# One core, attention twice and an MLP: the hand-written order of steps replaced by another, and the output tiles in a pool of five buffers

## The chip, the cores and the metric

The kernel runs on one core of one Trainium2 chip. The metric is the device time of one execution in microseconds (us), median over runs. TensorE is called PE here, VectorE DVE, ScalarE ACT, GpSimd POOL and SyncE SP.

## What is computed

Eight batches with eight heads each, 576 rows per batch. A small set of 32 rows `p` per head first attends to the keys and values; its result then serves as keys and values for all 576 rows of `q`. The result, 4608 x 512, goes through an MLP with a hidden width of 2048.

```python
def sm_attn(qq, kk, vv):
    s = scale * np.matmul(qq, kk.transpose(0, 1, 3, 2))
    s = s - np.max(s, axis=-1, keepdims=True)
    a = np.exp(s)
    a = a / (np.sum(a, axis=-1, keepdims=True) + 1e-09)
    return np.matmul(a, vv)
p_packed = sm_attn(p, k, v)
out = sm_attn(q, p_packed, p_packed)
...
h = x @ w_in
r = np.maximum(h, 0.0)
g = s * (r * r) + b
return (g @ w_out).astype(np.float32)
```

## The kernel before

The work is cut into steps, each a small function, and a long string of words (lines 581 to 614) says in which order the steps are written into the program. A word is a letter, a batch and, where there are parts, a part. All instructions are pinned: each engine runs its own in the order of the words and waits, in order, for what an instruction needs. The words, with what PE does in each:

- `Lk`, `Lv`, `Lq`, `Lwi`, `Lwo`, `Lpall`, `Lsb` load from HBM through POOL's queue (lines 108 to 140). `kn`, `vn` and `qn` have one buffer each, so the load of a batch waits until the one before has been used up.
- `Tk`, `Tq` (batches 0 and 1) transpose k and q on PE, half a batch each, 12 matmuls, and DVE copies the result out. `Dk`, `Dq` (batches 2 to 7) do it by a DMA transpose in SP's queue instead (line 204), from `kn` and `qn` into `kT` and `qT`.
- `V` reorders `vn` into `vr` on DVE. `PP` and `PPA` bring `p` of batch 0 and of the others into `pbd`.
- `F` (a=0, 1) are the first scores, 12 matmuls out of `kT`, and an exp on ACT. `P` (two halves, 18 small matmuls each) multiplies by `vr`; after the second half DVE and ACT copy the result by turns into `ppd`. `S` are the second scores, 16 matmuls, with two exps on ACT.
- `A` (two) makes the softmax weights `aT`: 2 matmuls, `ld` and `rcd` on ACT, one product on DVE. `W` multiplies the small attention result by W_in (16 matmuls, 8 in batch 0); ACT and DVE each evacuate one half into `pw`.
- `M` (16 per batch, `h` are halves of one) is the MLP's first layer: 4 matmuls out of `pw` and `aT`, a relu on ACT (in batch 0, every fourth on DVE, line 399), the square into `gT` on DVE.
- `O b.t xn` does n of the 16 matmuls of output tile t of batch b; after the last one DVE writes `ysb` (line 451) and SP stores it with two DMAs. `B` are 16 matmuls of the bias. `Z` are matmuls on zeros that nobody reads.

Two places matter for the order. PSUM has two buffers `hps` (line 57) through which all of T, F, P, S, A, W and M go in turn: the next step but one waits until ACT or DVE have read the tile. `ysb` comes from a pool with three buffers (line 55): the fourth tile to be written waits until the store of the first has landed.

```python
ysp = ctx.enter_context(tc.tile_pool(name="ysp", bufs=3))
psh = ctx.enter_context(tc.tile_pool(name="psh", bufs=2, space=bass.MemoryType.PSUM))
...
self.ysb = ysp.tile([P, NB], F32, tag="ysb", name="ysb")
```

Of the kernel before, what the change touches and what calls it, by code (L numbers as in the profile page):

```python
# [14 lines left out]
def kernel(  # L15
# [565 lines left out]
    for word in """
        Lwi3 Lwi0 Lwi2 Lwi1 Lwo0 Lwo1 Lpall Tk0.0 Z3 Tk0.1 Lk1 Lwo2 Lsb PP0 V0.0 Z6 F0.0 V0.1 Z4 F0.1
        Tq0.0 P0.0 P0.1 Tq0.1 Lq1 Lv1 Lwo3 Z5 S0 Z7 A0.0 Z1 W0.0 Z6 A0.1 Z1 h0.0.0 h0.1.0 Z6 h0.0.1
        h0.1.1 Z1 W0.1 M0.2 W0.2 B0-3 M0.3 B3-4 W0.3 O0.0x3 M0.4 B4-8 PPA M0.5 O0.0x2 O0.1x5 O0.2x3
        Tk1.1 M0.6 B8-12 Tk1.0 Lk2 M0.7 O0.0x2 F1.0 Tq1.0 O0.0x1 O0.1x1 M0.8 O0.1x1 Tq1.1 V1 Lv2 Lq2
        O0.1x1 F1.1 O0.0x1 O0.1x1 M0.9 O0.2x2 P1.0 P1.1 B12-16 S1 O0.0x1 O0.1x1 O0.2x2 M0.10 A1.0 O0.2x3
        W1.0 O0.0x1 O0.1x1 O0.2x1 V2 O0.3x3 M0.11 O0.3x3 A1.1 W1.2 O0.0x1 Dq2 Dk2 Lk3 Lv3 Lq3 O0.1x1
        O0.2x1 O0.3x2 M0.12 O0.3x2 M1.0 O0.3x2 M0.13 O0.0x1 M1.1 O0.1x1 O0.2x1 M0.14 O0.0x1 O0.1x1 M1.2
        O0.2x1 O0.3x1 M0.15 F2.0 O0.0x1 O0.1x1 M1.3 F2.1 O0.0x1 O0.1x1 O0.2x2 M1.4 P2.0 O0.3x1 P2.1
        O0.3x2 O1.0x1 M1.5 O1.0x1 S2 O1.0x4 O1.1x1 V3 M1.6 O1.1x1 A2.0 O1.1x2 W2.0 O1.0x1 O1.1x3 O1.2x1  # L590
        M1.7 Dq3 Dk3 Lk4 Lv4 Lq4 O1.2x3 A2.1 W2.2 O1.0x1 O1.1x1 O1.2x4 M1.8 O1.3x3 M2.0 O1.3x1 M1.9
        O1.0x1 O1.1x1 M2.1 F3.0 O1.0x1 O1.1x1 M1.10 O1.2x1 M2.2 O1.2x1 F3.1 O1.0x1 M1.11 O1.1x1 O1.2x1
        M2.3 P3.0 P3.1 M1.12 O1.0x1 O1.1x1 O1.2x1 S3 O1.3x1 O1.0x1 O1.1x1 V4 O1.2x1 O1.3x1 M2.4 O1.3x1
        M1.13 O1.3x3 M1.14 M2.5 Dq4 Dk4 Lk5 Lv5 Lq5 O1.0x1 O1.1x1 O1.2x1 O1.3x1 M1.15 M2.6 O1.0x1 O1.1x1
        O1.2x1 O1.3x1 W3.0 O1.0x1 O1.1x1 O1.2x1 O1.3x3 M2.7 A3.0 O1.3x1 O1.4x2 W3.2 O1.4x6 M2.8 O1.4x5
        A3.1 F4.0 O1.4x2 M2.9 O1.4x1 O2.0x3 F4.1 O2.0x1 M3.0 O2.0x1 M2.10 O2.0x1 P4.0 O2.0x1 P4.1 M2.11
        O2.0x1 S4 V5 O2.0x4 M2.12 Dq5 Dk5 Lk6 Lv6 Lq6 M3.1 O2.1x3 M2.13 O2.0x1 M3.2 O2.1x3 M2.14 O2.0x1
        M3.3 O2.1x3 M2.15 O2.0x1 M3.4 O2.1x2 F5.0 A4.0 O2.0x1 O2.1x3 W4.0 O2.1x2 O2.2x4 A4.1 O2.2x7 W4.2
        O2.2x5 M4.0 F5.1 O2.3x2 M3.5 O2.3x1 P5.0 O2.3x1 M4.1 P5.1 O2.3x3 Dq6 Dk6 Lk7 O2.3x3 V6 Lv7 Lq7
        O2.3x1 M4.2 M3.6 O2.3x2 S5 O2.3x3 O3.0x1 M4.3 O3.0x1 M3.7 O3.0x3 M4.4 O3.0x1 M3.8 O3.0x1 F6.0  # L600
        O3.0x1 M4.5 O3.0x1 M3.9 F6.1 O3.1x2 M4.6 O3.0x1 M3.10 O3.1x1 P6.0 M4.7 P6.1 O3.0x1 O3.1x6 M3.11
        V7 O3.1x2 M4.8 O3.2x2 M3.12 O3.0x1 O3.1x1 M4.9 M3.13 Dq7 Dk7 O3.0x1 O3.1x1 O3.2x2 M4.10 M3.14
        O3.0x1 O3.1x1 O3.2x2 M4.11 O3.2x1 M3.15 O3.0x1 O3.1x1 O3.2x1 M4.12 O3.2x1 A5.0 O3.0x1 O3.1x1
        W5.0 O3.2x6 M4.13 O3.2x1 O3.3x8 W5.2 O3.3x6 A5.1 M4.14 O3.3x2 F7.0 O3.4x5 S6 O3.4x5 F7.1 O3.4x5
        P7.0 O3.4x1 P7.1 M5.0 O4.0x7 M5.1 O4.0x7 M5.2 O4.0x1 M4.15 O4.1x3 M5.3 O4.1x1 A6.0 O4.0x1 O4.1x1
        W6.0 O4.1x5 M5.4 O4.1x6 A6.1 M5.5 O4.2x7 S7 O4.2x4 M6.0 O4.2x2 M5.6 O4.2x2 M6.1 O4.2x1 O4.3x1
        M5.7 O4.3x2 M6.2 O4.3x3 M5.8 O4.3x1 M6.3 O4.3x3 M5.9 O4.3x1 M6.4 O4.3x3 M5.10 M6.5 O4.3x2 O5.0x1
        M5.11 M6.6 O5.0x3 M5.12 M6.7 O5.0x3 M5.13 O5.0x6 M5.14 O5.0x1 O5.1x5 M5.15 O5.0x1 O5.1x5 A7.0
        O5.0x1 O5.1x6 W7.0 O5.2x13 W7.2 O5.2x3 O5.3x16 W6.2 O5.4x7 M6.8 O5.4x7 M6.9 O5.4x2 A7.1 O6.0x3
        M6.10 O6.0x6 M7.0 M6.11 O6.0x2 O6.1x2 M7.1 O6.1x1 M6.12 O6.0x1 O6.1x1 M7.2 M6.13 O6.0x1 O6.1x2  # L610
        M7.3 M6.14 O6.0x1 O6.1x2 M7.4 O6.1x1 M6.15 O6.0x1 O6.1x2 M7.5 O6.1x1 O6.0x1 O6.1x4 O6.2x1 M7.6
        O6.2x7 M7.7 O6.2x5 M7.8 O6.2x3 O6.3x2 M7.9 M7.10 O6.3x3 M7.11 M7.12 O6.3x6 M7.13 O6.3x5 O7.0x2
        M7.14 O7.0x7 M7.15 O7.0x6 O7.1x1 O7.0x1 O7.1x15 O7.2x16 O7.3x16 O7.4x16
    """.split():
# [31 lines left out]
```

## Time and profile before

| | us |
|---|---|
| median of 3 runs (288.86 to 289.34) | 288.96 |
| the profiled execution | 288.51 |
| its span, from the first to the last instruction | 286.7 |
| PE busy in it | 252.0 (88%) |
| ACT busy | 148.5 (52%) |
| DVE busy | 143.4 (50%) |

PE is the engine to look at; the others are about half used. The mean busy share hides what happens in time: PE works without a gap from about 187 us to the end, and has gaps before. Its clock was granted in full except in two of the 40 slices of the page, at about 72 to 79 and 136 to 143 us, after the two longest gaps. What has to be read, then, is each place where a matmul waits, what ended that wait, and what PE does from the start of one step to the start of the next.

### The profile page before, as it was taken

Reading aid. Unit: us, or ns where it says so; the run is one execution under the profiler, and the core shown is the slowest. Engines: PE = TensorE matmul, PEld = TensorE weight load, DVE = VectorE, ACT = ScalarE, POOL = GpSimd, SP = SyncE. Lnnn points to the kernel's source line nnn. Section 1 sums busy time; section 2 is a strip of 40 time slices with the busy share of each in tenths; the row PEclk is TensorE's granted clock in tenths of the full one; section 3 lists DMA queues with packets and bytes.
Section 4 is the critical chain, followed back from the end, with each engine's and each line's share of the span. In section 5 each row is a group of like instructions: output and inputs, shape, how many; then the busy total and the mean of one; then the engine's idle time right before and its main releaser. Section 6 shows DMA issues by size and latency. Waiting matters only on the chain.

```text
span 286.7 us, 5273 instructions
## 1 busy us (share of the span) xinstructions
PE 252.0 (88%) x2143; PEld 140.3 (49%) x2182; DVE 143.4 (50%) x274; ACT 148.5 (52%) x229; POOL 29.7 (10%) x44
## 2 busy tenths in 40 slices
...
PEclk9999999999699999999699999999999999999999
...
GB/s 79 182 206 207 195 203 161 143 164 118 259 123 80 203 143 173 222 87 164 121 235 121 155 183 130 129 64 30 74 39 37 0 112 48 26 75 37 64 85 73
DMA packets 59209, 35.48 MB, mean 124 GB/s; under 512 B 31920, under 2 KB 54704, under 8 KB 59184
## 3 DMA queue, kind: packets, MB, share of 16 engines
...
## 4 chain that ended last, share of the span: by engine, by line
PE 62%; DMA 20%; ACT 7%; DVE 6%; issue 3%; POOL 1%; SPq 1%; POOLq 0%; ACTq 0%; DVEq 0%
PE yps L61 34%; PE hps L61 25%; DMA vn<-in_v_dram 8%; DMA kT<-kn 7%; ACT rlu L72 3%; DMA out_dram<-ysb 2%; DMA kn<-in_k_dram 2%; PE zps L61 2%; DVE gT L72 1%; PE hps L64 1%; ACT pw L72 1%; ACT ld L72 1%; DVE pw L72 1%; DVE pbd L72 1%; DVE ysb L72 1%
## 5 line engine op out<-in xcount | busy, mean ns | idle before, releaser
L61 PE MATMUL yps<-w_out_sb,gT 128*128 128x512 bf16 (+1 forms) x559 | 144.7, 379 | 8.5 <-DVE gT L72 6.7
L72 ACT ACTIVATE rlu<-hps 128x576 bf16<-128x576 f32 x122 | 78.1, 651 | 58.1 <-PE hps L61 50.2
L72 DVE TENSOR_TENSOR gT<-rlu 128x576 bf16<-128x576 bf16 x126 | 57.3, 457 | 67.9 <-ACT rlu L72 66.4
L61 PEld LDWEIGHTS <-gT 128*128 128x128 bf16 x592 | 55.4, 99 | 57.4 <-DVE gT L72 9.5
L61 PE MATMUL hps<-aT,pw 128*128 128x288 bf16 x512 | 82.1, 287 | 0.7 <-DVE pw L72 0.2
L61 PEld LDWEIGHTS <-pw 128*128 128x128 bf16 x512 | 49.7, 98 | 32.6 <-issue 4.2
L72 DVE SCALAR_TENSOR_TENSOR ysb<-yps,svec,biasrep 128x512 f32<-128x512 f32 (+1 forms) x37 | 26.5, 733 | 23.7 <-PE yps L61 16.8
L72 ACT ACTIVATE pw<-hps,rd 128x1024 bf16<-128x1024 f32 (+1 forms) x18 | 18.4, 1020 | 13.3 <-PE hps L61 13.1
...
L72 DVE TENSOR_TENSOR aT<-e,rcd 128x576 bf16<-128x576 bf16 x16 | 12.1, 758 | 23.5 <-ACT rcd L72 21.7
L72 DVE TENSOR_SCALAR pw<-hps,rd 128x1024 bf16<-128x1024 f32 (+1 forms) x18 | 20.9, 1161 | 2.3 <-PE hps L61 1.2
...
L61 PE MATMUL hps<-pbd,kT 128*128 128x64 bf16 x192 | 8.5, 196 | 9.0 <-DMA kT<-kn 7.1
L61 PE MATMUL zps<-zb 128*128 128x512 bf16 x49 | 14.3, 427 | 1.4 <-DVE zb L72 1.2
L61 PE MATMUL hps<-w_in_sb,ppd 64*32 64x512 bf16 x256 | 13.1, 405 | 2.5 <-DVE pw L72 1.0
...
L61 PEld LDWEIGHTS <-kT 128*128 128x128 bf16 x192 | 7.7, 100 | 12.7 <-DMA kT<-kn 8.2
L72 ACT ACTIVATE ld<-hps 128x576 f32<-128x576 f32 x16 | 10.4, 650 | 6.6 <-PE hps L61 6.6
L72 ACT ACTIVATE e<-hps,rs 128x576 bf16<-128x576 f32 (+1 forms) x18 | 11.3, 686 | 1.5 <-PE hps L61 1.5
...
L72 ACT ACTIVATE rcd<-ld 128x576 f32<-128x576 f32 x16 | 11.0, 685 | 0.5
L72 ACT CAST ppd<-hps 64x128 bf16<-64x128 f32 x16 | 4.2, 261 | 12.9 <-DVE ppd L72 12.1
...
## 6 DMA issues: line engine op xcount, KB each, us to landing
...
qn<-in_q_dram POOLq DMA_DIRECT2D x7, 576.0 KB, 13.2
...
```

The costliest lines, as they stand in the source:

```text
L61: return tc.keep_in_program_order(nc.tensor.matmul(*a, **kw))
L64: return tc.keep_in_program_order(nc.tensor.transpose(*a, **kw))
L72: return lambda *a, **kw: tc.keep_in_program_order(f(*a, **kw))
```

## The change

Three things. The string of words is another one, with the same steps in another order and other numbers of `Z` (59 matmuls on zeros in place of 52). `ysb` gets a pool of its own with five buffers. The order of the first loads differs. The steps themselves are unchanged.

```diff
     ysp = ctx.enter_context(tc.tile_pool(name="ysp", bufs=3))
+    outp = ctx.enter_context(tc.tile_pool(name="outp", bufs=5))
...
-                self.ysb = ysp.tile([P, NB], F32, tag="ysb", name="ysb")
+                self.ysb = outp.tile([P, NB], F32, tag="ysb", name="ysb")
...
-        Lwi3 Lwi0 Lwi2 Lwi1 Lwo0 Lwo1 Lpall Tk0.0 Z3 Tk0.1 Lk1 Lwo2 Lsb PP0 V0.0 Z6 F0.0 V0.1 Z4 F0.1
-        Tq0.0 P0.0 P0.1 Tq0.1 Lq1 Lv1 Lwo3 Z5 S0 Z7 A0.0 Z1 W0.0 Z6 A0.1 Z1 h0.0.0 h0.1.0 Z6 h0.0.1
...
+        Lwi1 Lwi0 Lwo0 Lwi2 Lwi3 Lwo2 Lwo1 Lpall Tk0.0 Z10 Tk0.1 PP0 Z6 F0.0 V0.0 F0.1 V0.1 Z5 P0.0
+        Tq0.0 P0.1 Z4 Tq0.1 Lq1 Lk1 Lwo3 Lv1 Lsb Z3 S0 Z7 A0.0 A0.1 Z2 W0.0 Z3 W0.1 B0-4 Z7 h0.0.0
...
-        O2.0x1 S4 V5 O2.0x4 M2.12 Dq5 Dk5 Lk6 Lv6 Lq6 M3.1 O2.1x3 M2.13 O2.0x1 M3.2 O2.1x3 M2.14 O2.0x1
-        M3.3 O2.1x3 M2.15 O2.0x1 M3.4 O2.1x2 F5.0 A4.0 O2.0x1 O2.1x3 W4.0 O2.1x2 O2.2x4 A4.1 O2.2x7 W4.2
...
+        O2.3x3 W4.0 O2.3x4 W4.2 V5 O2.3x6 S4 O2.3x3 O3.0x1 A4.0 O3.0x2 A4.1 O3.0x2 Dq5 Dk5 Lk6 Lv6 Lq6
+        M3.15 O3.0x10 M4.0 M4.1 O3.0x1 O3.1x1 M4.2 M4.3 O3.1x2 M4.4 M4.5 O3.1x2 M4.6 M4.7 O3.1x2 M4.8
+        F5.0 O3.1x2 F5.1 O3.1x1 M4.9 O3.1x2 P5.0 M4.10 P5.1 O3.1x4 O3.2x3 W5.0 O3.2x6 W5.2 O3.2x6 S5
```

For batches 2, 4 and 5 both `W` now stand ahead of `S`, with output steps between; `Dq` and `Dk` of the next batch come after `A`; then the `M` come two at a time with two output steps between pairs, and `F` of the next batch stands near the end of that row. For batches 0, 1, 3, 6 and 7 the steps are spread in other ways.

SP's queue from its start. Before, the first transposes (`qT`, `kT` of batch 2) stood ahead of all stores of output tiles (`out_dram<-ysb`):

```order
L72 DMA_TRANSPOSE qT_87<-qn 128x24x96
L72 DMA_TRANSPOSE kT_85<-kn 128x24x96
L72 DMA out_dram<-ysb 96x512
L72 DMA out_dram<-ysb 32x512
L72 DMA out_dram<-ysb 64x512 x2
```

Now the same queue from its start:

```order
L73 DMA out_dram<-ysb 96x512
L73 DMA out_dram<-ysb 32x512
L73 DMA out_dram<-ysb 64x512 x2
L73 DMA out_dram<-ysb 32x512
L73 DMA out_dram<-ysb 96x512
L73 DMA_TRANSPOSE qT_90<-qn 128x24x96
L73 DMA_TRANSPOSE kT_88<-kn 128x24x96
```

The transposes of batch 2 have moved behind the six stores of the first three output tiles.

DVE around `P2`, `S2` and `V3` (`rd`, `ppd`, `rs` are what follows `P2`; `vr` is `V3`). Before:

```order
L72 SCALAR_TENSOR_TENSOR ysb<-yps,svec,biasrep 128x512 x3
L72 TENSOR_TENSOR gT<-rlu 128x576
L72 RECIPROCAL rd<-hps 128x2
L72 CAST ppd_90<-hps 64x128 x2
L72 TENSOR_SCALAR rs<-rd 128x2
L72 SCALAR_TENSOR_TENSOR ysb<-yps,svec,biasrep 128x512
L72 TENSOR_TENSOR gT<-rlu 128x576
L72 COPY vr<-vn 96x8x6x64
```

Now the same place:

```order
L73 TENSOR_TENSOR gT<-rlu 128x576 x11
L73 RECIPROCAL rd<-hps 128x2
L73 CAST ppd_93<-hps 64x128 x2
L73 TENSOR_SCALAR rs<-rd 128x2
L73 TENSOR_SCALAR pw<-hps,rd 128x1024 x2
L73 COPY vr<-vn 96x8x6x64
L73 TENSOR_TENSOR aT<-e_1183,rcd 128x576
```

Four writes of `ysb` that stood close to `P2` and ahead of `V3` are gone from there; both evacuations of `W2` now stand between `P2` and `V3`, and the weights `aT` of batch 2 follow `V3`.

## Rows read from the trace of the kernel before

**Rows 1.** Page, part 2: granted PE clock in 40 slices, tenths.

```profile
PEclk9999999999699999999699999999999999999999
```

**Rows 2.** Waits: engine line <- waited for: us in total, times, longest us.

```profile
DVE ysb L72 <- DMA out_dram<-ysb: 6.8, 2, 4.5
```

**Rows 3.** Timeline of PE: start us, us, engine, what, count, [idle before <-releaser].

```profile
75.97 1.04 PE L61 MATMUL yps<-w_out_sb,gT 128*128 128x512 bf16 x2 [3.83 <-DVE gT L72]
...
113.41 0.51 PE L61 MATMUL hps<-pbd,kT 128*128 128x64 bf16 x12 [1.87 <-DVE pw L72]
...
126.23 0.39 PE L61 MATMUL yps<-w_out_sb,gT 128*128 128x512 bf16 x1 [1.73 <-DVE gT L72]
...
136.03 0.82 PE L61 MATMUL hps<-pbd,kT 128*128 128x64 bf16 x12 [4.80 <-DMA kT<-kn]
...
159.65 0.52 PE L61 MATMUL hps<-pbd,kT 128*128 128x64 bf16 x12 [1.95 <-DMA kT<-kn]
```

**Rows 4.** Windows: length, busy us (instructions) of PE, PEld, DVE, ACT, POOL; clock, DMA.

```profile
76.40:82.00 5.60, 5.49 (x33) 2.19 (x33) 3.10 (x4) 3.10 (x4) 0.00 (x0) 0.66 0.65 130
...
136.10:145.00 8.90, 8.68 (x67) 3.45 (x69) 4.43 (x6) 4.86 (x7) 2.30 (x3) 0.69 0.91 132
```

**Rows 5.** Timeline of PE and ACT, late in the span, without waits between.

```profile
227.59 0.63 PE L61 MATMUL hps<-w_in_sb,ppd 64*32 64x512 bf16 x16
228.15 2.98 PE L61 MATMUL yps<-w_out_sb,gT 128*128 128x512 bf16 x12
...
248.60 1.14 PE L61 MATMUL hps<-aT,pw 128*128 128x288 bf16 x8
249.29 1.19 ACT L72 ACTIVATE rlu<-hps 128x576 bf16<-128x576 f32 x2 [0.43 <-PE hps L61]
249.58 0.81 PE L61 MATMUL yps<-w_out_sb,gT 128*128 128x512 bf16 x3
...
250.22 0.65 PE L61 MATMUL hps<-aT,pw 128*128 128x288 bf16 x4
...
267.66 15.53 PE L61 MATMUL yps<-w_out_sb,gT 128*128 128x512 bf16 x86
```

**Rows 6.** Timeline from 26 us: the first full `M`, `PPA` on PE, ACT's share of it.

```profile
26.20 0.66 PE L61 MATMUL hps<-aT,pw 128*128 128x288 bf16 x4
...
33.09 0.96 PE L64 MATMUL hps<-identb,pall 112*128 112x112 bf16 x16 [0.71 <-DVE pall L72]
...
36.26 1.71 ACT L72 COPY pbd<-hps 64x896 bf16<-64x896 bf16 x2 [4.05 <-DVE pbd L72]
```

**Rows 7.** Timeline of SP and POOL: transposes, and the loads that follow them.

```profile
89.93 0.78 POOL L72 DMA_DIRECT2D kn<-in_k_dram  x1 [22.96 <-issue]
...
101.86 2.89 SPq L72 DMA_TRANSPOSE qT<-qn  x1
...
110.55 0.77 POOL L72 DMA_DIRECT2D kn<-in_k_dram  x1 [18.31 <-DMA kT<-kn]
...
127.78 3.06 SPq L72 DMA_TRANSPOSE qT<-qn  x1
```

**Rows 8.** The chain that ended last: start us, us, what (a DMA to its landing).

```profile
104.84 5.15 DMA kT<-kn
...
111.31 13.52 DMA vn<-in_v_dram
```

**Rows 9.** Timeline of all engines after `P2`, and the two evacuations of a `W`.

```profile
68.33 0.29 PE L61 MATMUL hps<-ones,e 96*128 96x1 bf16 x6
...
69.03 0.17 DVE L72 RECIPROCAL rd<-hps 128x2 f32<-128x2 f32 x1
...
70.08 0.26 ACT L72 CAST ppd<-hps 64x128 bf16<-64x128 f32 x1 [0.36 <-DVE ppd L72]
...
70.39 0.32 PE L61 MATMUL hps<-qT,ppd 64*32 64x288 bf16 x8 [0.61 <-ACT ppd L72]
...
80.99 1.28 DVE L72 TENSOR_SCALAR pw<-hps,rd 128x1024 bf16<-128x1024 f32 x1
```

More of the change, by code (lines that the diff above doesn't have):

```diff
@@ L581 @@
     for word in """
-        Lwi3 Lwi0 Lwi2 Lwi1 Lwo0 Lwo1 Lpall Tk0.0 Z3 Tk0.1 Lk1 Lwo2 Lsb PP0 V0.0 Z6 F0.0 V0.1 Z4 F0.1
-        Tq0.0 P0.0 P0.1 Tq0.1 Lq1 Lv1 Lwo3 Z5 S0 Z7 A0.0 Z1 W0.0 Z6 A0.1 Z1 h0.0.0 h0.1.0 Z6 h0.0.1
-        h0.1.1 Z1 W0.1 M0.2 W0.2 B0-3 M0.3 B3-4 W0.3 O0.0x3 M0.4 B4-8 PPA M0.5 O0.0x2 O0.1x5 O0.2x3
-        Tk1.1 M0.6 B8-12 Tk1.0 Lk2 M0.7 O0.0x2 F1.0 Tq1.0 O0.0x1 O0.1x1 M0.8 O0.1x1 Tq1.1 V1 Lv2 Lq2
-        O0.1x1 F1.1 O0.0x1 O0.1x1 M0.9 O0.2x2 P1.0 P1.1 B12-16 S1 O0.0x1 O0.1x1 O0.2x2 M0.10 A1.0 O0.2x3
@@ L587 @@
[L587 to L596, printed above, removed]
@@ L597 @@
-        O2.0x1 S4 V5 O2.0x4 M2.12 Dq5 Dk5 Lk6 Lv6 Lq6 M3.1 O2.1x3 M2.13 O2.0x1 M3.2 O2.1x3 M2.14 O2.0x1
-        M3.3 O2.1x3 M2.15 O2.0x1 M3.4 O2.1x2 F5.0 A4.0 O2.0x1 O2.1x3 W4.0 O2.1x2 O2.2x4 A4.1 O2.2x7 W4.2
-        O2.2x5 M4.0 F5.1 O2.3x2 M3.5 O2.3x1 P5.0 O2.3x1 M4.1 P5.1 O2.3x3 Dq6 Dk6 Lk7 O2.3x3 V6 Lv7 Lq7
-        O2.3x1 M4.2 M3.6 O2.3x2 S5 O2.3x3 O3.0x1 M4.3 O3.0x1 M3.7 O3.0x3 M4.4 O3.0x1 M3.8 O3.0x1 F6.0
-        O3.0x1 M4.5 O3.0x1 M3.9 F6.1 O3.1x2 M4.6 O3.0x1 M3.10 O3.1x1 P6.0 M4.7 P6.1 O3.0x1 O3.1x6 M3.11
@@ L602 @@
[L602 to L611, printed above, removed]
@@ L612 @@
-        O6.2x7 M7.7 O6.2x5 M7.8 O6.2x3 O6.3x2 M7.9 M7.10 O6.3x3 M7.11 M7.12 O6.3x6 M7.13 O6.3x5 O7.0x2
-        M7.14 O7.0x7 M7.15 O7.0x6 O7.1x1 O7.0x1 O7.1x15 O7.2x16 O7.3x16 O7.4x16
+        Lwi1 Lwi0 Lwo0 Lwi2 Lwi3 Lwo2 Lwo1 Lpall Tk0.0 Z10 Tk0.1 PP0 Z6 F0.0 V0.0 F0.1 V0.1 Z5 P0.0
+        Tq0.0 P0.1 Z4 Tq0.1 Lq1 Lk1 Lwo3 Lv1 Lsb Z3 S0 Z7 A0.0 A0.1 Z2 W0.0 Z3 W0.1 B0-4 Z7 h0.0.0
+        h0.0.1 h0.1.0 h0.1.1 M0.2 O0.0x1 M0.3 O0.0x1 O0.1x1 M0.4 M0.5 O0.0x2 M0.6 M0.7 O0.1x3 O0.2x1
+        W0.2 W0.3 O0.2x2 M0.8 O0.2x1 M0.9 B4-12 PPA M0.10 O0.0x6 O0.1x3 Tq1.0 O0.1x1 Tq1.1 O0.0x1 O0.1x1
@@ new lines @@
+        Tk1.0 O0.1x1 Tk1.1 Lk2 O0.1x1 M0.11 O0.2x1 M0.12 B12-16 F1.0 F1.1 O0.0x2 O0.1x1 V1 Lv2 Lq2 M0.13
+        O0.1x1 M0.14 O0.2x1 P1.0 P1.1 O0.0x1 M0.15 O0.0x1 O0.1x2 S1 O0.2x1 O0.0x1 O0.1x1 O0.2x1 A1.0
+        O0.2x3 W1.0 O0.2x1 V2 O0.2x4 O0.3x1 A1.1 O0.3x4 W1.2 O0.3x3 Dq2 Dk2 Lk3 Lv3 Lq3 O0.3x4 M1.0
+        O0.3x3 M1.1 M1.2 O0.3x1 O1.0x1 M1.3 M1.4 O1.0x2 M1.5 M1.6 O1.0x2 M1.7 M1.8 O1.0x2 M1.9 M1.10
+        O1.0x1 F2.0 O1.0x1 M1.11 O1.0x2 F2.1 M1.12 O1.0x1 O1.1x2 P2.0 M1.13 P2.1 O1.0x1 O1.1x3 O1.0x1
@@ new lines @@
+        O1.1x2 W2.0 O1.1x6 W2.2 O1.1x1 O1.2x5 V3 S2 O1.2x5 A2.0 O1.2x2 M1.14 M1.15 O1.2x2 O1.3x2 A2.1
+        O1.3x1 Dq3 Dk3 Lk4 Lv4 Lq4 O1.3x1 O1.0x1 O1.1x1 O1.0x1 O1.1x1 O1.2x2 O1.3x3 M2.0 M2.1 O1.3x2
+        M2.2 M2.3 O1.3x2 M2.4 M2.5 O1.3x2 M2.6 M2.7 O1.3x2 M2.8 F3.0 O1.3x1 O1.4x1 F3.1 O1.4x1 M2.9
+        O1.4x2 P3.0 M2.10 P3.1 O1.4x6 S3 O1.4x5 A3.0 O1.4x1 O2.0x1 A3.1 O2.0x2 M2.11 O2.0x3 M2.12 O2.0x3
+        V4 O2.0x1 W3.0 O2.0x3 O2.1x3 M2.13 O2.1x2 M3.0 M3.1 O2.0x1 O2.1x1 Dq4 Dk4 Lk5 Lv5 Lq5 M3.2 M3.3
@@ new lines @@
+        O2.1x2 M3.4 M3.5 O2.1x2 M3.6 M3.7 O2.1x2 M2.14 M2.15 O2.1x2 W3.2 O2.0x2 O2.1x2 O2.2x3 M3.8 M3.9
+        O2.2x2 M3.10 M3.11 O2.2x2 M3.12 F4.0 O2.2x2 F4.1 O2.2x1 M3.13 O2.2x2 P4.0 M3.14 P4.1 O2.2x4
+        O2.3x3 W4.0 O2.3x4 W4.2 V5 O2.3x6 S4 O2.3x3 O3.0x1 A4.0 O3.0x2 A4.1 O3.0x2 Dq5 Dk5 Lk6 Lv6 Lq6
+        M3.15 O3.0x10 M4.0 M4.1 O3.0x1 O3.1x1 M4.2 M4.3 O3.1x2 M4.4 M4.5 O3.1x2 M4.6 M4.7 O3.1x2 M4.8
+        F5.0 O3.1x2 F5.1 O3.1x1 M4.9 O3.1x2 P5.0 M4.10 P5.1 O3.1x4 O3.2x3 W5.0 O3.2x6 W5.2 O3.2x6 S5
@@ new lines @@
+        O3.2x1 O3.3x1 V6 O3.3x2 A5.0 O3.3x2 A5.1 O3.3x2 M4.11 O3.3x3 M4.12 O3.3x4 Dq6 Dk6 Lk7 Lv7 Lq7
+        M4.13 M4.14 O3.3x2 M4.15 O3.4x16 O4.0x1 M5.0 M5.1 O4.0x2 M5.2 M5.3 O4.0x2 M5.4 M5.5 O4.0x2 M5.6
+        M5.7 O4.0x2 M5.8 M5.9 O4.0x2 M5.10 M5.11 O4.0x2 M5.12 M5.13 O4.0x2 M5.14 M5.15 O4.0x1 O4.1x1
+        F6.0 O4.1x1 F6.1 O4.1x5 P6.0 P6.1 O4.1x4 V7 O4.1x1 W6.0 O4.1x4 O4.2x2 S6 Dq7 Dk7 O4.2x3 A6.0
+        O4.2x3 A6.1 O4.2x8 W6.2 O4.3x6 M6.0 O4.3x3 M6.1 M6.2 O4.3x2 M6.3 M6.4 O4.3x5 M6.5 M6.6 O5.0x2
```

5 lines of the change are left out of this document (added).

## Prediction

> **What bounds the kernel now.** I read the granted clock first, then the waits, then PE's timeline at each wait, then SP and POOL. PE is the engine that sets the end: from about 187 us it runs without a gap. So the time is PE's work plus what PE loses before that. The work is the words of the code at the full clock, each from the start of a step to the start of the next. Two `M` take 0.98 (248.60 to 249.58), so one is 0.49; three `O` steps take 0.64 to 0.65, so one is 0.216; a `W` is 0.56 [rows 5]. The same reading gives 0.35 for an `F`, 0.50 for a half `P`, 0.40 for `S`, 0.245 for `A`, 0.50 for a `T`. Counted over the string before: 128 `M` 62.7, 36 output tiles 124.4, bias 3.5, 52 `Z` 11.2, `F` 5.6, `P` 8.1, `S` 3.2, `A` 3.9, `W` 9.0, `T` 4.0, `PP` and `PPA` 0.7, together 236.3. The last matmul ends at 267.66 + 15.53 = 283.2 [rows 5]; **PE loses 46.9 us**. After it come 3.5 us of the last `ysb` and its store.
>
> Following each step's start minus the work ahead of it, the loss stands at 8.7 when `M0.2` starts at 26.20 [rows 6], 14.3 after `S1` (49.4), 16.1 at `F2`, 23.7 at 81.8, 28.6 at `F4`, 32.0 at 131.1, 40.0 at 145.0, 42.8 at `F6`, 44.6 at 172.2, 46.9 at the end. The large pieces have names. At 75.97 PE had waited 3.83 for `gT`, which stood on DVE behind a `ysb` that waited up to 4.5 for a store, since there are three buffers [rows 2, 3]. At 113.41 `F4` waited 1.87 for a `pw` evacuation queued behind the second such `ysb` [rows 2, 3]. At 126.23 it was 1.73, DVE being stuck at `V5`. `F5` waited 4.80 and `F6` 1.95 for the DMA transpose of k [rows 3]. After the two waits of about 4 and 5 us the granted clock was 0.66 and 0.69 for 5.6 and 8.9 us [rows 1, 4], part of it at the lower of its two levels: (1 - 0.66) x 5.6 = 1.9 and (1 - 0.69) x 8.9 = 2.8 lost again.
>
> **The change, part by part.** I take my own sum as: work 236.3 plus 7 more `Z` (1.5), plus the new losses, stage by stage.
>
> *Five buffers.* They remove the two waits on stores: 3.83 + 1.9 + 1.87 = 7.6. A tile now waits for the store five tiles back, and between those lie over 20 us of PE work, while the stores wait at most for one pair of transposes in SP's queue. I cost it at nothing; if a store were that late, the wait of before would be back, 4.5 each.
>
> *Transposes.* `Dq` and `Dk` share SP; the second is issued 3.0 after the first and lands 5.15 after that (101.86, 104.84) [rows 7, 8], so `F` can start 8.15 after `Dq`. PE's work between the place of `Dq` and `F` in the string was 6.7, 6.0, 9.6, 6.5, 6.8, 13.2 for batches 2 to 7; now it is 8.8, 8.3, 11.0, 8.8, 16.9, 29.2. That removes 4.80 + 2.8 + 1.95 and 0.5 at `F2`, if `Dq` starts when the string comes to it. It waits for `qn`. The three loads of a batch can start when `Dk` has landed and took 11.9 (89.93 to 101.86, no stores meanwhile) to 17.2 (110.55 to 127.78, eight stores) [rows 7]. A round is therefore 0.6 + 11.9 to 17.2 + 8.15 = 20.7 to 26.0. PE's work from `Dq` to the next `Dq` is 22 to 23 plus 1.5 to 2 lost, say 24.5. The two chains run level; the DMA chain has the worse end. Batch by batch, with six to eight stores in a load, I find `F3` 2 us, `F4` 6, `F5` 1 and `F6` 8 or more behind their `kT`; a worst load takes 2 us from that, so I put nothing there, and keep 0 to 2 each open on `F3` and `F5`. The one I do charge is `F2`: its transposes moved behind six stores, `O0.2` is written at about 60.7, two more issues make 62.0, `kT` lands at 70.1, PE arrives at 69.7: 0.4.
>
> *`V`.* In the worst round `vn` landed 14.3 after the load of k was issued (110.55 to 111.31 + 13.52), in the others earlier [rows 7, 8]. `V3` to `V7` come 8 to 14 us after it, and behind each of them but `V4` DVE has 1 to 9 us until PE needs what it does next, so the 1.73 of `V5` and 1.2 of `V7` go; on the other side `V4`, with `W3.0` right behind it, could lose 2.
>
> *Start, to `S1`.* Loads up to `qn` are unchanged and set the same pace. `Tq0.1` now takes the `hps` tile of `P0` and waits about 1.0 for `ppd`; both `A0` stand ahead of `W0`, so ACT does two `ld` and `rcd` before the first `pw`. I follow it to `M0.2` at 27.4 (before: 26.20), with 0.9 of bias work and 1.5 of `Z` more done: loss 7.5. Then `W0.2` and `W0.3` back to back make `M0.8` wait for `pw`: 1.2. `PPA` is evacuated by DVE and ACT one after the other, until 37.97, 4.9 after its first matmul [rows 6]; PE has 0.6 + 0.49 + 9 x 0.216 = 3.0 of work in that, so 1.9 are lost before `Tq1.0`, where it was 1.5. On POOL `Lsb` went to the end of the first loads; the same bytes as before stand ahead of it, the last of them landed at 46.4, and the bias needs it at 47.7: nothing, or up to 1 if the loads run later. `S1` waits 1.1 for `ppd` and a relu, and 0.3 go in smaller waits. Loss at `S1` 12.0, against 14.3. From there to `F2` small waits of 0.6 and the 0.4: 13.0.
>
> *Batches 2 to 7.* After `P` the copies into `ppd` take 1.3 (69.03 to 70.34), and the whole from the end of `P` to `S` was 1.9 [rows 9]. With the new `M` between the two halves of `P`, the square of that `M` (relu 0.69 after its start, 0.65, then 0.46) stands ahead of them on DVE: about 2.15 in all, with 1.3 to 1.5 of `O` steps as cover. Wait 0.75, between 0.4 and 0.9. `W` to the next `W` needs 0.2 + 1.28 of evacuation [rows 9]; the cover is 1.30 where six or seven `O` steps stand, 0.86 in batch 4: 0.25, there 0.7. `F` among pairs of `M` loses 0.3 to ACT. Sums: batch 2 1.4, batch 3 2.0 (it has a `W` inside the row of `M`, 0.5), batch 4 1.95, batch 5 1.5, batch 6 0.9, batch 7 0.8; and 0.1 for each of 13 `W`, 1.3. Together 9.85.
>
> *Pairs of `M`.* A tile is free 0.69 + 0.65 after its `M` starts, and a second relu starts 0.54 after the first (249.29, two in 1.19) [rows 5]. In a pair with two `O` steps (period 1.41) the next pair's second `M` comes 1.90 after the first of this one and its tile is free at 1.88. It fits by 0.02; 0 to 0.05 for each of 46 pairs, I take 0.5.
>
> The losses are 13.0 + 9.85 + 0.5 = 23.4. Against before: 46.9 - 23.4 = 23.5 less, 1.5 of `Z` more, so **-22.0**. The profiled execution, 288.51, becomes 266.5; the median of the runs is 0.45 above it, so 267.0.
>
> **The rivals.**
> *One or two long waits remain.* The load chain is level with PE. If loads take the 17 us of the worst round twice, or the stores, now in groups behind the transposes, stretch them further, `F3`, `F5` or `V4` wait 3 to 4 us and bring the lower clock: 3.5 + 2.4 each by [rows 3, 4]. One to two of them: 273 to 279. For it speaks the round of 26.0, against it that three of five rounds before were under 24.
> *The small waits don't add up.* Waits in a row hide one another: what `P` loses, the transposes and `V` gain. Without half of the 9.85 and of the start's gain lost: 259 to 262.
> *The clock.* The rows of `M` pairs are full of short PE stops. In the stretches of before with many stops below 2 us the clock stayed full [rows 1]. The Trainium skill, TensorE: Matmul & The Clock Gate, section "A second HAM failure mode: psum-queue depth-cycling", has short idles between matmul groups take the clock down and up again; by that rule, the trace so far does not agree. As a mechanism of this kernel its price is one fall per batch, 2.4 as after the gaps above: 6 x 2.4 = 14, 281.
> *Slower than before.* `V` and `F` of every batch come late. If stores and loads together make a round 29 us or more, `F3` to `F6` and `V4` wait over 4 us each and each pays the clock: 5 x (4.5 + 2.4) = 34, 301. It decides from a round of about 27.5, above any of the five seen.
> *It does nothing.* Then 289; the order on SP and DVE does differ, so this needs the losses to come back one for one.
>
> **How the numbers follow.** Forecast as worked out (263 to 271) 0.62; long waits remain 0.17; small waits hidden 0.14; clock 0.02; slower 0.03; nothing 0.02. The range leaves out the upper part of the long waits, the clock, the slow cases and the lower end of the hidden ones: 259 to 277. A run of this kernel can tell about 0.2% from no change. Faster 0.95, same 0.015, slower 0.035.
>
> **What would show it.** PE's granted clock is full after the start in all slices. No `ysb` waits for a store. `F3` to `F7` start with no wait on `kT`; `F2` waits under 1 us. `M0.2` starts near 27.4 and `S1` ends near 54.3. Waits of 0.3 to 0.9 stand at the first `W` or `S` after each `P`. Wrong would be a wait of over 2 us on `kT` or `vn` in any batch, a low clock in a slice, or a start that loses more than 14 at `S1`.

## The result, and the profile after

The changed kernel takes 264.14 us (median of 4 runs, 263.85 to 265.76) against 288.91 before (4 runs), a ratio of 0.917 with a 95% interval of 0.911 to 0.922. The forecast was 267.0, with a range of 259 to 277. The profiled execution took 264.41, its span is 262.6. The number came out; the experiments show that one of its larger entries, the 7.6 for the five buffers, had no ground. The forecast did not hang on it, since it was added up from the losses expected in the new order and not from the waits that would go.

The page of the kernel after, busy time and PE's granted clock in 40 slices:

```profile
span 262.6 us, 5259 instructions
...
PE 247.5 (94%) x2152; PEld 140.5 (53%) x2189; DVE 144.0 (55%) x274; ACT 143.8 (55%) x229; POOL 29.7 (11%) x44
...
PEclk9999999999999999999999999999999999999999
```

The two low slices of [rows 1] are gone. PE's work counted over the words is now 237.8 (7 more `Z`), and it loses 21.3 us by the reading of the prediction, where it lost 46.9.

PE's timeline, start, duration, what, and the wait ahead of it, at the first `F` of batches 2 to 6; they answer to [rows 3]:

```profile
69.62 0.52 PE L62 MATMUL hps<-pbd,kT 128*128 128x64 bf16 x12 [0.37 <-DMA kT<-kn]
...
93.15 0.51 PE L62 MATMUL hps<-pbd,kT 128*128 128x64 bf16 x12
...
120.64 0.51 PE L62 MATMUL hps<-pbd,kT 128*128 128x64 bf16 x12
...
143.31 0.52 PE L62 MATMUL hps<-pbd,kT 128*128 128x64 bf16 x12 [0.94 <-DMA kT<-kn]
...
175.33 0.51 PE L62 MATMUL hps<-pbd,kT 128*128 128x64 bf16 x12
```

The waits of 4.80 and 1.95 have become 0.94 and none. On DVE, `V3` to `V7` start with no wait for the load of `vn`, which stood ahead of four of them before. First that wait in the kernel before (us in total, times, longest), then the first four `V` now:

```profile
DVE vr L72 <- DMA vn<-in_v_dram: 7.3, 4, 3.3
```

```profile
80.37 0.96 DVE L73 COPY vr<-vn 96x3072 bf16<-96x3072 bf16 x1
105.31 0.95 DVE L73 COPY vr<-vn 96x3072 bf16<-96x3072 bf16 x1
130.73 0.94 DVE L73 COPY vr<-vn 96x3072 bf16<-96x3072 bf16 x1
154.73 0.95 DVE L73 COPY vr<-vn 96x3072 bf16<-96x3072 bf16 x1
```

The whole change can be read from one table: for each `F`, the PE work of the words ahead of it, when its `kT` landed (from the records of the DMAs), and when it started.

| batch | work ahead of F, before | after | kT landed, before | after | F started, before | after |
|---|---|---|---|---|---|---|
| 2 | 48.0 | 57.1 | 64.1 | 69.6 | 64.1 | 69.6 |
| 3 | 64.6 | 79.6 | 88.8 | 91.2 | 89.2 | 93.2 |
| 4 | 84.8 | 105.2 | 110.0 | 115.6 | 113.4 | 120.6 |
| 5 | 99.0 | 125.1 | 136.0 | 143.3 | 136.0 | 143.3 |
| 6 | 116.9 | 156.1 | 159.6 | 165.6 | 159.7 | 175.3 |

From the landing of batch 2 to that of batch 6 the DMAs need 95.5 us before and 96.0 after. **The transfers have not become faster; each lands later than before.** In those 95.5 us the old order has 116.9 - 48.0 = 68.9 of PE work to do. The new order has 99.0 between the same two `F`. I call this theory D: the loads of a batch wait for its predecessor's transposes, the transposes wait for the loads, and this chain runs through the middle of the program at about 24 us a round, whatever PE does; an order gains there by what it puts ahead of `F` and `V`. The records of the DMAs bear it out for the order before: the pairs of batches 2 to 7 each went out within 0.1 us of the landing of their `qn`, and the loads of batches 3 to 7 0.5 to 1.1 after the `kT` of the batch before had landed. In the new order the pairs of batches 3, 4 and 6 do the same; those of 2, 5 and 7 go out 1.6, 3.1 and 5.7 after `qn`, so the place of `Dq` in the string moves the chain as well.

### The profile page after: what moved, and what is told of

It is laid out like the page before. It is cut to its first block, busy times and chain, and to the rows that moved or that the text cites. A ratio compares the mean times of both kernels' runs of the same rounds, so it can differ in the third digit from the quotient of the medians.

```text
span 262.6 us, 5259 instructions
## 1 busy us (share of the span) xinstructions
PE 247.5 (94%) x2152; PEld 140.5 (53%) x2189; DVE 144.0 (55%) x274; ACT 143.8 (55%) x229; POOL 29.7 (11%) x44
## 4 chain that ended last, share of the span: by engine, by line
PE 76%; DMA 12%; ACT 4%; DVE 4%; issue 2%; POOL 0%; SPq 0%; POOLq 0%; ACTq 0%
PE yps L62 43%; PE hps L62 31%; DMA w_out_sb<-in_moe_w_out_dram 5%; DMA kT<-kn 4%; DMA kn<-in_k_dram 2%; ACT rlu L73 2%; DVE gT L73 1%; ACT ppd L73 1%; DVE ppd L73 1%; PE hps L65 1%; ACT pw L73 1%; ACT pbd L73 1%; PE zps L62 1%; DVE pbd L73 0%; ACT rluh L73 0%
## 5 line engine op out<-in xcount | busy, mean ns | idle before, releaser
L62 PE MATMUL yps<-w_out_sb,gT 128*128 128x512 bf16 (+1 forms) x558 | 138.3, 373 | 1.9 <-DVE gT L73 0.3
L73 ACT ACTIVATE rlu<-hps 128x576 bf16<-128x576 f32 x122 | 74.0, 648 | 35.4 <-PE hps L62 35.1
L62 PEld LDWEIGHTS <-gT 128*128 128x128 bf16 x592 | 54.8, 97 | 49.8 <-issue 6.3
L62 PE MATMUL hps<-aT,pw 128*128 128x288 bf16 x512 | 76.5, 285 | 2.1 <-ACT rluh L73 1.1
L73 ACT ACTIVATE e<-hps 96x768 bf16<-96x768 f32 x16 | 12.2, 803 | 20.9 <-PE hps L62 20.7
L73 DVE TENSOR_SCALAR pw<-hps,rd 128x1024 bf16<-128x1024 f32 (+1 forms) x18 | 20.7, 1161 | 4.3 <-PE hps L62 3.4
L62 PE MATMUL zps<-zb 128*128 128x512 bf16 x56 | 16.1, 427 | 1.5 <-DVE zb L73 1.2
L62 PEld LDWEIGHTS <-zb 128*128 128x128 bf16 x59 | 5.8, 107 | 8.1 <-issue 3.2
L62 PEld LDWEIGHTS <-vr 96*128 96x128 bf16 x192 | 7.6, 98 | 2.7 <-issue 0.9
```

Source lines behind the costliest of these rows:

```text
L73: return lambda *a, **kw: tc.keep_in_program_order(f(*a, **kw))
```

## Experiments

### The five buffers alone, in either order

```diff
+    outp = ctx.enter_context(tc.tile_pool(name="outp", bufs=5))
-                self.ysb = ysp.tile([P, NB], F32, tag="ysb", name="ysb")
+                self.ysb = outp.tile([P, NB], F32, tag="ysb", name="ysb")
```

This is the old order with five buffers; the second run is the new order with `bufs=3` in that pool.

> The order of steps before, with ysb in a pool of five buffers: the buffers alone. By the prediction's sum the two waits on stores and the clock lost behind the first go: 3.83 + 1.9 + 1.87 = 7.6 less, about 281.3. Rival: in the old order the loads and transposes set the pace of the middle of the program, not PE; then what PE gains at 76 and 113 us is waited away again at the next F, since kT of batches 3 to 6 does not land earlier. That gives 286 to 289, with the waits of F5 and F6 on kT longer than the 4.80 and 1.95 of before, or a new one at F3 or F4.

> The new order with three output buffers as before: what the buffers are worth there. In the old order a ysb waited up to 4.5 because the stores were queued behind a transposing pair. In the new one the stores also stand around the pair Dq, Dk, and a tile waits for the store three back, some 10.4 us of PE work (3 tiles of 3.46) instead of 17. Theory (the order made the buffers necessary): ysb waits for a store once or more, 1 to 4 us each, 266 to 272. Rival (the order already separates the stores from the pairs, the buffers only take an insurance): no wait on a store that delays PE, 264.1 within 0.5.

The old order with five buffers took 289.04, ratio 0.9997 (0.997 to 1.002): nothing of the 7.6. The new order with three took 264.52, 0.4 above 264.14, within the spread of either. In both runs it came to the rival's time, though not in every sign: in the old order `F5` was to wait longer than 4.80 and waited 3.04. The store behind the longer wait of before, 4.55 at 74.80, was not queued behind a pair, as the second text has it: its two DMAs were issued at 67.46 and 67.87 and had landed at 74.67, while the loads of batch 3 ran. The trace of the old order with five buffers shows where the gain went; first the waits (engine, what it waited for, us in total, times, longest), then the timeline of DVE and PE:

```profile
DVE vr L73 <- DMA vn<-in_v_dram: 12.9, 3, 5.8
```

```profile
76.55 0.96 DVE L73 COPY vr<-vn 96x3072 bf16<-96x3072 bf16 x1 [5.79 <-DMA vn<-in_v_dram]
77.43 0.45 DVE L73 TENSOR_TENSOR gT<-rlu 128x576 bf16<-128x576 bf16 x1
...
77.93 1.61 PE L62 MATMUL yps<-w_out_sb,gT 128*128 128x512 bf16 x5 [3.66 <-DVE gT L73]
...
125.34 0.39 PE L62 MATMUL yps<-w_out_sb,gT 128*128 128x512 bf16 x1 [3.48 <-DVE gT L73]
...
135.05 0.52 PE L62 MATMUL hps<-pbd,kT 128*128 128x64 bf16 x12 [3.04 <-DMA kT<-kn]
...
158.72 0.82 PE L62 MATMUL hps<-pbd,kT 128*128 128x64 bf16 x12 [4.25 <-DMA kT<-kn]
```

No `ysb` waits for a store any more, and PE still stops 3.66 at 77.93, where it stopped 3.83 before. Next in DVE's queue stood `V3`, and `vn` of batch 3 landed at 76.53. Further on, the 1.87 of `F4` is gone, `V5` costs 3.48 in place of 1.73, `F5` 3.04 in place of 4.80 and `F6` 4.25 in place of 1.95. At `F7` the loss stands at 45.3, as before.

### Start and rest, exchanged

Two strings were joined at `Dk2`: the words of one order up to it, then the words of the other that were not yet written, in their sequence. The new start with the old rest, against the new order:

```diff
         W1.2 O0.3x3 Dq2 Dk2 Lk3 Lv3 Lq3
-        O0.3x4 M1.0 O0.3x3 M1.1 M1.2 O0.3x1 O1.0x1 M1.3 M1.4 O1.0x2
+        O0.3x2 M1.0 O0.3x2 M1.1 M1.2 O0.3x1 F2.0 M1.3 F2.1 M1.4 P2.0
```

The old start with the new rest, against the old order:

```diff
         W1.2 O0.0x1 Dq2 Dk2
-        Lk3 Lv3 Lq3 O0.1x1 O0.2x1 O0.3x2 M0.12 O0.3x2 M1.0 O0.3x2 M0.13
+        M0.12 O0.0x1 O0.1x1 M0.13 O0.1x1 M0.14 O0.0x1 M0.15 O0.0x1 O0.1x2
```

> The other way round: the words of the new order up to and with Dk2, then the words of before, five output buffers. Theory D: the start gains nothing, it costs. In the new start the pair of batch 2 goes out 5 us later (61.0 for 55.9), and the old rest waits for that chain at F3 to F6, so F6 starts about 5 later than before: 293 to 295. Rival (gains of the parts add): the start alone is worth 14.3 - 11.5 = 2.8 less 1.5 of Z, 287.6, within 0.7.

> The words of before up to and with Dk2, from there the words of the new order (those not yet written, in the new order's sequence), five output buffers. It asks where the 24.8 us lie. Theory D (the loads and transposing pairs form one chain, and the new order gains because F of batches 3 to 6 stands behind more PE work, so that kT and vn are there): nearly all lies behind Dk2. At the cut PE has lost 15.5 against 11.9 in the new order, with 1.5 fewer Z; and the pair of batch 2 goes out about 5 earlier, which takes the waits of F2 and F5 (0.5 and 1.1): 264.1 + 2.0 - 1.6 = 264 to 265. Rival (gains of the parts add, each on its own): 264.1 + 2.0 = 266 or more, F5 still waiting.

The new start with the old rest took 293.37, ratio 1.015 (1.009 to 1.021): 4.5 us slower than before, as theory D has it. PE's timeline there, at `F2` and `F5`:

```profile
69.58 0.82 PE L62 MATMUL hps<-pbd,kT 128*128 128x64 bf16 x12 [6.38 <-DMA kT<-kn]
...
139.44 0.82 PE L62 MATMUL hps<-pbd,kT 128*128 128x64 bf16 x12 [4.73 <-DMA kT<-kn]
```

At the end of `S1` PE has lost 2.9 less than in the old start (11.4 for 14.3). All of it, and more, is waited away at `F2`, since the new start sends the first pair of transposes 5 us later.

The old start with the new rest took 272.55, ratio 0.943 (0.938 to 0.948), 6.5 to 8.5 above both expectations. Much of that is the joint: four `M` of batch 0 come there one by one with one or two output steps between. PE stops twice, and from the second stop on its granted clock is low (the second block has the columns of [rows 4]):

```profile
57.07 0.65 PE L62 MATMUL hps<-aT,pw 128*128 128x288 bf16 x4 [0.90 <-ACT pw L73]
58.95 1.04 PE L62 MATMUL yps<-w_out_sb,gT 128*128 128x512 bf16 x2 [1.24 <-DVE gT L73]
```

```profile
57.50:65.00 7.50, 6.26 (x22) 2.38 (x20) 2.97 (x6) 1.95 (x3) 0.77 (x2) 0.54 0.77 141
65.00:68.00 3.00, 3.00 (x15) 1.44 (x16) 2.07 (x3) 0.00 (x0) 1.52 (x2) 1.00 0.77 88
```

```profile
150.39 0.52 PE L62 MATMUL hps<-pbd,kT 128*128 128x64 bf16 x12 [1.60 <-DMA kT<-kn]
```

The loss goes from 14.7 to 20.2 over the joint; the two stops are 2.1 of it, and nearly all the rest is the clock, 0.54 in the mean for 7.5 us, most of that at the lower of its two levels (1.2 GHz). The clock did not fall like that in every run: one with a mean granted clock of 1.000 took 270.93, still 4.9 above the rival's 266, and that remainder is not explained. Behind the joint the new rest loses another 9.6, against 9.4 in the new kernel (11.9 at the same place, 21.3 at the end of the last matmul). So the rest of the program loses between 9 and 10 in the new words; in the old ones it loses 31 (15.5 to 46.9), and 36 behind the new start. `F5`, which I had expected free of its wait here, waits 1.60.

### One wait taken away in the old order

```diff
-        O2.1x2 F5.0 A4.0 O2.0x1 O2.1x3 W4.0 O2.1x2 O2.2x4 A4.1 O2.2x7 W4.2 O2.2x5 M4.0 F5.1
+        O2.1x2 A4.0 O2.0x1 O2.1x3 W4.0 O2.1x2 O2.2x4 A4.1 O2.2x7 W4.2 O2.2x5 M4.0 F5.0 F5.1
```

The second run has this, and the first scores and `P` of batch 6 later as well: `F6.0 M4.7 O3.0x1 F6.1 O3.1x6 P6.0 M3.11 P6.1` where `P6.0` stood.

> The order before (three output buffers) with one word moved: F5.0 from ahead of A4.0 to right ahead of F5.1, that is behind 6.9 us more of PE work. Theory D (one chain of loads and transposing pairs): the wait of 4.80 at F5 and the low clock behind it go, but kT of batch 6 lands at 159.6 as before, since its loads start when kT of batch 5 has landed (136.0) whatever PE does; F6 then starts at 159.6 all the same, after a wait of 8 to 10 instead of 1.95. Time 288.5 to 291. Rival (each wait is its own term, as the prediction summed them): 4.80 + 2.8 less, 281.

> The same, and F6.0, F6.1, P6.0, P6.1 later too: F6.0 behind 3.2 us more of PE work than before. Theory D: F6 starts at 159.6 again with 3.2 more done, so the gain is 3.2 and nothing more, 285 to 286.5. Rival (independent waits): 4.80 + 2.8 + 1.95 less, 279.

Moving `F5.0` gave 289.95, ratio 1.003 (0.999 to 1.007), within theory D's bounds. PE at `F5` and at `F6`:

```profile
139.01 0.51 PE L61 MATMUL hps<-pbd,kT 128*128 128x64 bf16 x12
...
160.34 0.82 PE L61 MATMUL hps<-pbd,kT 128*128 128x64 bf16 x12 [8.73 <-DMA kT<-kn]
```

`F5` no longer waits, and `F6` waits 8.73 for 1.95. The longest wait of the kernel before is gone, and the time is the same.

With `F6` later too it took 288.53, ratio 0.999 (0.995 to 1.004); I had expected 285 to 286.5. The profiled execution was the longest of the ten, 292.34, and began 2.2 us late (its `F2` starts at 66.3), so I read differences. From `F2` to `F6` PE loses 23.6, where it lost 26.7 before: the 3.2 are there. Then, on PE, DVE and PE:

```profile
161.97 0.82 PE L61 MATMUL hps<-pbd,kT 128*128 128x64 bf16 x12 [4.44 <-DMA kT<-kn]
...
172.58 0.96 DVE L72 COPY vr<-vn 96x3072 bf16<-96x3072 bf16 x1 [2.81 <-DMA vn<-in_v_dram]
...
174.33 1.04 PE L61 MATMUL yps<-w_out_sb,gT 128*128 128x512 bf16 x4 [2.32 <-DVE gT L72]
```

The windows behind the two waits, columns as in [rows 4]:

```profile
162.00:167.00 5.00, 5.00 (x55) 3.34 (x56) 0.46 (x1) 2.26 (x3) 2.30 (x3) 0.66 0.75 111
174.00:180.00 6.00, 5.67 (x26) 3.13 (x27) 2.02 (x5) 2.53 (x4) 0.00 (x0) 0.72 0.59 109
```

`V7` is the next thing that hangs from the same chain. It cost PE 1.15 before and costs 2.32 here; `P6` at its new place loses another 0.6. The clock takes the larger part: granted in full in both windows before, it was 0.66 and 0.72 here, (1 - 0.66) x 5 + (1 - 0.72) x 6 = 3.4. From `F6` to `F7` PE loses 7.3 in this execution, where it lost 2.5 before; whether the faster runs lost the 3.2 in the same way no trace shows. My expectation looked at `F` alone and forgot that `V` needs the same loads.

### Loads sent ahead of the transposes

If the single buffers of `kn` and `qn` tie the loads to the transposes, two buffers each should cut the chain (`vn` keeps one):

```diff
+    kqp = ctx.enter_context(tc.tile_pool(name="kqp", bufs=2))
...
-            raw[what, b] = rawp.tile([R, H, NC * D], BF16, tag=what + "n", name=what + "n")
+            raw[what, b] = (rawp if what == "v" else kqp).tile([R, H, NC * D], BF16, tag=what + "n", name=what + "n")
```

> The order before, five output buffers, and kn and qn with two buffers each (vn keeps one), so that loads of k and q need not wait until the transposes of the batch before have landed. Theory A (waits on transposes come from the late load of qn and kn): Dq and Dk start when the string comes to them, and F5 and F6 lose their 4.80 and 1.95 and the low clock; 281.3 - 4.8 - 2.8 - 2 = about 271 to 273. Theory B (they come from where Dq and Dk stand in the string, too close ahead of F): the pair still needs 8.15 from Dq to F against 6 to 7 us of PE work, so F5 and F6 wait 1 to 2 each, no low clock, 275 to 279.

> The order before, three output buffers, kn and qn with two buffers each: the fourth corner of the square of order before with 3 or 5 output buffers, and 1 or 2 buffers of kn and qn. If the two edits act alone, this gains over the kernel before what the doubled kn and qn gain on top of five output buffers (8 to 10, so 279 to 281). If the stores are what holds the transposes and the transposes what holds the stores, both stay late together and it gains under 4, 285 to 289.

> The new order with kn and qn in two buffers each. In the two runs of the old order with this edit the loads of the next batch ran beside the transposing pair, and a DMA transpose took 9 to 13 instead of 5. Theory (one buffer keeps loads and transposes apart, which is worth more than an early load): the pairs of batches 2 to 5 take 4 to 8 longer, F2 to F5 wait 3 to 9 each with the low clock behind, 272 to 285. Rival (an early load takes qn off the chain, as in theory A of the old order): F2 and F5 lose their waits, 262.5 to 263.5.

The old order with five output buffers took 289.71 (286.92 to 292.41), ratio 0.996 (0.990 to 1.002), with three 292.02, ratio 1.010 (1.007 to 1.014). Of the theories for the old order none held. The new order took 283.04, ratio 0.976 (0.968 to 0.985): 19 us slower than without the second buffers, as the third expectation has it; of the four long waits that it lists, at `F2` to `F5`, only those of `F2` and `F5` came. The reason stands in the DMA view, transposes with their count and median us from issue to landing. The kernel before:

```profile
qT<-qn SPq DMA_TRANSPOSE x6, 5.1
kT<-kn SPq DMA_TRANSPOSE x6, 5.1
```

The kernel after:

```profile
qT<-qn SPq DMA_TRANSPOSE x6, 5.3
kT<-kn SPq DMA_TRANSPOSE x6, 5.0
```

The old order with five output buffers and two of `kn` and `qn`:

```profile
qT<-qn SPq DMA_TRANSPOSE x6, 6.6
kT<-kn SPq DMA_TRANSPOSE x6, 8.3
```

The new order with two of `kn` and `qn`, and PE's waits in it at `F2` and `F5`:

```profile
qT<-qn SPq DMA_TRANSPOSE x6, 11.6
kT<-kn SPq DMA_TRANSPOSE x6, 8.9
```

```profile
76.84 0.82 PE L63 MATMUL hps<-pbd,kT 128*128 128x64 bf16 x12 [7.52 <-DMA kT<-kn]
...
158.29 0.82 PE L63 MATMUL hps<-pbd,kT 128*128 128x64 bf16 x12 [6.06 <-DMA kT<-kn]
```

Pairs that run beside the loads of the next batch take longer: at the medians 1.3 and 1.6 times as long in the old order, 2.2 and 1.8 times in the new. The single buffer holds the chain together, and it also keeps its two kinds of transfers apart.

### The waits that the new order still has

SP's timeline in the kernel after, at the transposes of batches 2 and 5:

```profile
61.01 3.62 SPq L73 DMA_TRANSPOSE qT<-qn  x1
64.69 2.98 SPq L73 DMA_TRANSPOSE kT<-kn  x1
...
133.67 3.64 SPq L73 DMA_TRANSPOSE qT<-qn  x1
137.40 3.61 SPq L73 DMA_TRANSPOSE kT<-kn  x1
```

`qn` had landed at 59.4 and at 130.6. And PE around the first `M` and the two `W` in a row:

```profile
26.36 0.65 PE L62 MATMUL hps<-aT,pw 128*128 128x288 bf16 x4 [0.50 <-ACT rluh L73]
27.56 0.90 PE L62 MATMUL hps<-aT,pw 128*128 128x288 bf16 x6 [0.55 <-ACT rluh L73]
...
34.86 0.65 PE L62 MATMUL hps<-aT,pw 128*128 128x288 bf16 x4 [0.84 <-DVE pw L73]
```

Three edits of the string. Transposes early, ahead of the store:

```diff
-        O0.2x1 V2 O0.2x4 O0.3x1 A1.1 O0.3x4 W1.2 O0.3x3 Dq2 Dk2 Lk3 Lv3 Lq3
+        O0.2x1 V2 Dq2 Dk2 O0.2x4 O0.3x1 A1.1 O0.3x4 W1.2 O0.3x3 Lk3 Lv3 Lq3
...
-        V5 O2.3x6 S4 O2.3x3 O3.0x1 A4.0 O3.0x2 A4.1 O3.0x2 Dq5 Dk5 Lk6 Lv6 Lq6
+        V5 Dq5 Dk5 O2.3x6 S4 O2.3x3 O3.0x1 A4.0 O3.0x2 A4.1 O3.0x2 Lk6 Lv6 Lq6
```

Half steps by turns:

```diff
-        h0.0.0 h0.0.1 h0.1.0 h0.1.1 M0.2
+        h0.0.0 h0.1.0 h0.0.1 h0.1.1 M0.2
```

Both of these, and `W0.2` ahead of `M0.6`:

```diff
-        M0.4 M0.5 O0.0x2 M0.6 M0.7 O0.1x3 O0.2x1 W0.2 W0.3
+        M0.4 M0.5 O0.0x2 W0.2 M0.6 M0.7 O0.1x3 O0.2x1 W0.3
```

> The new order with Dq2 Dk2 right behind V2 and Dq5 Dk5 right behind V5, that is ahead of the store of one output tile in SP's queue; the loads stay where they are. In the trace of the new order Dq5 started at 133.67, behind that store, though qn had landed at 130.58, and F5 lost 1.1; Dq2 started at 61.01 with qn landed at 59.44, and F2 lost 0.5. Theory: the place in SP's queue set both waits; the pairs start 1.5 and 2.6 earlier, both waits go, 1.6 less: 262.5. Rival: the pair then runs beside stores or is slower, or the chain of loads takes it back at a later F: 263.6 to 264.1.

> The new order with the four half steps of M0.0 and M0.1 by turns (h0.0.0 h0.1.0 h0.0.1 h0.1.1) instead of one after the other. In the trace of the new order the second half of each waited some 0.7 for the relu of the first half, which is in the same tile. Theory: both waits go, since PE does the half of the other tile meanwhile: 0.7 to 1.4 less, about 263.1, if nothing in the loads takes it back. Rival: PE reaches F2 earlier and waits there longer for kT, no change, 264.1 within 0.3.

> The new order with the two edits that gained put together (half steps by turns; the pairs of batches 2 and 5 ahead of a store) and W0.2 moved ahead of M0.6, so that M0.8 need not wait 1.0 for the pw of two W in a row. If the three are independent: 0.9 + 1.0 + 0.8 less than the new order's 264.1, 261.4. Rival (what the start gains is waited for at F2, since qn of batch 2 lands at 59.4 whatever PE does): F2 waits 1 to 2, 262.3 to 262.8.

The early transposes took 262.63 (262.11 to 263.14), ratio to before 0.908 (0.905 to 0.912), 1.5 below the new order as expected. The pair of batch 5 goes out 4.6 earlier, and `F2` and `F5` have no wait:

```profile
129.10 2.90 SPq L73 DMA_TRANSPOSE qT<-qn  x1
```

```profile
69.32 0.51 PE L62 MATMUL hps<-pbd,kT 128*128 128x64 bf16 x12
...
141.90 0.51 PE L62 MATMUL hps<-pbd,kT 128*128 128x64 bf16 x12
```

The half steps by turns took 263.56 (262.78 to 263.87), ratio 0.912 (0.908 to 0.915). The two waits shrink to 0.25 and 0.20, and the loss at the end of the program is 1.1 smaller (20.2 for 21.3). The medians differ by 0.6, no more than the runs spread; the trace is the better witness here.

All three together took 263.01 (262.77 to 263.25), ratio 0.910 (0.906 to 0.914), no better than the early transposes alone. The rival had the time nearly right and the place wrong. `F2` waits for nothing; the gain of the half steps is lost ahead of it, at `M0.7`:

```profile
32.23 0.65 PE L62 MATMUL hps<-aT,pw 128*128 128x288 bf16 x4 [0.93 <-DVE pw L73]
```

`W0.2` holds one of the two `hps` tiles until DVE has evacuated it, wherever it stands. Moved, it made `M0.7` wait 0.93 and left 0.35 at `M0.9`, for the 0.84 at `M0.8`. The early transposes have the lowest median of all versions, 0.4 below this one, which is within the spread of either; early transposes and half steps together, with `W0.2` in its old place, were not tried.

## The prediction, point by point

**The base of the sum** held: PE sets the end, and its work and losses, read step by step, add up in both traces.

**The step that failed is "They remove the two waits on stores: 3.83 + 1.9 + 1.87 = 7.6", under "Five buffers".** Measured, they remove nothing. I followed each wait to what ended it, and did not ask what stood next. Behind the freed `ysb` stood `V3` on DVE, with `vn` landing at 76.8, and behind that `kT` of batches 5 and 6, whose times the chain had fixed. The prediction itself says that loads and transposes make a round of 20.7 to 26.0 and that "the two chains run level"; it used this for the order after, and costed the waits of before as if each were its own. The run with `F5` moved shows the same: 4.80 removed, 6.8 put on at `F6`. The total did not suffer. It was added up forward, from the losses of the new order, where the buffers stand at nothing, as they measured; the 7.6 only named a part of what was to go. And the new order clears the whole chain at once, so what was lost on it goes, under whichever name the profile had booked it.

**Transposes** were right in their main part. I placed the `F` of batches 3 to 6 at 2, 6, 1 and 8 or more behind their `kT`; measured were 2.0, 5.1, none and 9.8. `F2` waits 0.37 (forecast 0.4). `F5` lost 1.1 where I put nothing and kept 0 to 2 open: its pair stood behind a store in SP's queue, 3 us after `qn`, and the run with the pair ahead of that store has no wait.

**`V`** was right, and `V4` did not lose the 2 it could have.

**The start** was right in size, 11.5 at `S1` (forecast 12.0), and wrong in its bookkeeping. I counted it as 2.3 gained; with the old rest behind it, it costs 4.5. Of its parts, `M0.8` lost 1.0 (forecast 1.2). `Tq0.1` did not wait the 1.0 and `Tq1.0` lost 0.6 of 1.9: I let the two `hps` tiles go strictly by turns, while in the trace the wait of `Tq1.0` ends with the relu of `M0.10` and not with `pbd`: it took the tile that was let go first. Not foreseen were 0.6 on the first load of W_out, ahead of the bias, and 0.7 at each of two half steps that use a tile whose first half ACT was still reading.

**Batches 2 to 7** lost 1.1, 1.9, 1.6, 1.0, 0.95 and 1.1, together 7.7 for 9.85. The term too large was `W` after `P`: 0.75 forecast, 0.37 to 0.51 measured. PE's timeline after `P2`:

```profile
75.71 0.29 DVE L73 CAST ppd<-hps 64x128 bf16<-64x128 f32 x1 [0.38 <-ACT ppd L73]
75.88 0.27 PEld L62 LDWEIGHTS <-ppd 64*32 64x32 bf16 x2 [0.42 <-issue]
...
76.04 0.26 ACT L73 CAST ppd<-hps 64x128 bf16<-64x128 f32 x1 [0.36 <-DVE ppd L73]
```

`W2.0` starts before the last copy into `ppd` does, as it needs that part only for its later matmuls. **Pairs of `M`** lost nothing that can be told from the batches (forecast 0.5).

Together: start and `F2` -0.5, batches -2.2, pairs -0.5, `F5` +1.1, which makes 21.3 for 23.4 and 264.4 for 266.5 in the profiled execution. That the sum missed by only 2.1 is in part luck: `F5` came out 1.1 over, the others 3.2 under. **Of the rivals**, the small waits that hide one another came half true; the long waits, the low clock and the slower kernel did not come. The clock's premise did not come about: in the rows of `M` pairs PE hardly stops (from 164 to 176 it is busy 11.89 of 12.00 us, no stop above 0.06), and the granted clock is full in every slice. So the kernel after doesn't test that rival; in the old start with the new rest the granted clock did fall, around the last of three stops of 0.42, 0.90 and 1.24. The slower kernel needed rounds of over 27.5 all the way; one, from `kT` of batch 4 to that of batch 5, came to 27.7, and the others to 21.6, 24.4 and 22.3. Of the signs, that no `ysb` waits for a store needs a word: the profile books two such waits of 2.70, at 245.24 and 255.60, but the two `ysb` between them wait the same 2.70 for PE, which does not stop there.

Open is how much a store costs a transpose. The pair of batch 5 took 6.8 and 5.9 right behind a store of two DMAs, and 5.0 each ahead of it, in the run with early transposes; but other neighbours moved with it, and no run changed the stores alone. The pair of batch 4, with a store issued 3 us ahead, took 6.6 and 5.3.
